# First batch of an attention-plus-FFN kernel: turns, masks and value scaling placed anew

## The chip, the cores and the metric

One core of a Trainium2 chip runs the whole kernel. The metric is device time in microseconds (us) of one launch; medians are given, and every comparison is with runs of the kernel before on the same chip in the same session. Engines are named as in the profile: PE is TensorE (matmuls), ACT is ScalarE, DVE is VectorE, POOL is GpSimd, SP is SyncE.

## The reference, cut to what matters

Attention with a forget gate over 8 batches, 8 heads, 576 positions, 64 channels, and then a gated FFN over the 4608 tokens.

```python
def _attn_ref(q, k, v, f):
    scores = scale * np.matmul(q, k.transpose(0, 1, 3, 2))
    cum = np.cumsum(np.log(np.clip(f, 0.0001, 1.0)), axis=-1)
    scores = np.where(causal, -1000000000.0, scores + decay)   # decay from cum
    ...
    return np.matmul(softmax, v)
# FFN: (sigmoid(x @ w_gate) * (x @ w_val)) @ w_out
```

## The kernel before: the parts that the change touches

The kernel works on one batch after the other; within a batch on four pairs of heads. While batch b+1 is in attention, TensorE fills its time with the FFN of batch b. Only the first batch has no FFN beside it, and only the first batch's schedule is changed. I call the moment when the first transposes of the second batch start on TensorE the **hand-over**: what comes after it is the same in both kernels.

For each pair p of the first batch there are three score units U, V and W. One unit is: scores on TensorE, the exponential on ScalarE, the causal mask (`affine_select`) on GpSimd.

```python
def S_unit(p, u, slot, tag=None, e=None):
    ...                                    # score matmuls into PSUM
    nc.scalar.activation(e[:, :, 0:w], ps[:, sc:sc + 2, 0:w], ACTF.Exp, scale=scale)
    m, pat = diag(e)
    nc.gpsimd.affine_select(out=m, in_=m, compare_op=ALU.is_ge, fill=0.0,
                            base=0, pattern=pat, channel_multiplier=-1)

def vg_step(p, eng=None):                  # values times the gate; GpSimd unless told otherwise
    ...
def out_one(p, bs, bv):
    pair_region(p, 512 * bs, 0, MAIN, False)    # ten matmuls: sums of weights
    ...                                         # VectorE: transpose, reciprocal, spread
    yield
    pair_region(p, 512 * bv, 0, MAIN, True)     # ten matmuls: values (needs vg of p)
    scaled(p, 512 * bv, R, 0, MAIN)
    if p == 0:
        cross_x(p, 1, 0, MAIN)                  # exchange of halves by two transfers
def swap(p, bank):                              # the same exchange by TensorE and a ScalarE copy
    ...

main_unit(0, "U", 0)
for p in range(HPAIR):
    main_unit(p, "V", 1 - p % 2)
    if p + 1 < HPAIR:
        T_step(p + 1, 4, DVEC, ACTC)            # turn q and k of the next pair
    if p:
        burst = out_one(p - 1, 6, 7)
        next(burst)
    main_unit(p, "W", p % 2)
    if p == 0:
        load_qk(1, 0, ((0, 4),))
    elif p == 1:
        load_w1(512, 1024)
    if p > 1:
        vg_step(p)
    if p + 1 < HPAIR:
        main_unit(p + 1, "U", 1 - p % 2)
    if p == 0:
        vg_step(0, nc.vector)
        vg_step(1, nc.vector)
    if p:
        next(burst, None)
load_w1(1024, 1536)
swap(1, 0)
...                                             # FFN projections of the first batch begin
```

In what follows a *turn* is `T_step`, the transposes of one pair's q and k; a *burst* is `out_one`, and its two halves are the *sums* and the *values*; *vg* is the value scaling. The calls are in program order for every engine. `load_qk` and `load_w1` are issued by GpSimd too, two transfers each.

The softmax here doesn't subtract the row's maximum and nothing guards it: scores larger than these inputs give would overflow.

## Time and profile before

| | before |
|---|---|
| median | 374.01 us (373.73 to 374.12, 3 runs) |
| span in the profile | 372.6 us |
| first exponential | 8.85 us |
| pair 2's masks done | 19.53 us |
| hand-over | 28.07 us |
| from hand-over to end | 344.5 us |

The prediction shows the chain. The table of stretches gives, for each stretch in us, its length, the busy time of PE, PEld, DVE, ACT and POOL with instruction counts, then the clock share, the DMA share and GB/s:

```profile
16.80:21.60 4.80, 4.52 (x90) 2.96 (x88) 4.13 (x8) 4.61 (x6) 3.82 (x8) 1.00 1.22 210
21.60:28.10 6.50, 6.25 (x72) 2.80 (x69) 3.87 (x7) 2.60 (x5) 6.50 (x10) 1.00 1.24 210
100.00:200.00 100.00, 99.99 (x1694) 55.04 (x1692) 52.70 (x123) 54.09 (x82) 63.50 (x93) 1.00 1.12 159
```

From 16.8 us on TensorE has 0.5 us of slack before the hand-over, and almost none in the long stretch from 100 to 200 us. In GpSimd's timeline (start, length, engine, line, operation, operands) pair 2's three masks are these:

```profile
17.07 0.43 POOL L250 TENSOR_SCALAR_AFFINE_SELECT gv<-gv 128x256 bf16<-128x256 bf16 x1
18.04 0.64 POOL L250 TENSOR_SCALAR_AFFINE_SELECT gv<-gv 128x512 bf16<-128x512 bf16 x1 [0.54 <-ACT gv L248]
19.12 0.41 POOL L250 TENSOR_SCALAR_AFFINE_SELECT gv<-gv 128x256 bf16<-128x256 bf16 x1 [0.45 <-ACT gv L248]
```

The brackets say that GpSimd was idle before the second and third and waited for their exponentials. These two are as early as ScalarE allows; the first stands directly behind a weight load.

### The profile page before, as it was taken

The page shows a single profiled execution, that of the slowest core. Times are in us where ns is not written, and L with a number is a line of the kernel's source. Part 1 is how long each engine was busy: PE and PEld are TensorE (multiplying, and loading weights), DVE is VectorE, ACT ScalarE, POOL GpSimd, SP SyncE. Part 2 cuts the span into 40 slices and gives each one's busy share as a digit, 9 for nine tenths or more (in the row PEclk, how much of TensorE's full clock was granted, in tenths as well). Part 3 has the DMA queues.
Part 4 walks back from the last instruction along what each step waited for, and adds up shares of the span by engine and source line. Part 5 has one row for each costly group of instructions (what it writes and reads, how often), then busy time and mean ns, then how long its engine had stood idle before and what let it go on. Part 6 is the DMA issues. An engine that isn't in the chain of part 4 may idle for free.

```text
span 372.6 us, 12205 instructions
## 1 busy us (share of the span) xinstructions
PE 359.1 (96%) x5259; PEld 192.5 (52%) x5264; DVE 178.1 (48%) x382; ACT 195.6 (52%) x294; POOL 168.3 (45%) x265
## 2 busy tenths in 40 slices
PE   3899999999999999999999999999999999999996
PEld 1547645455645545454665556544456544444442
DVE  5875473557374755273617460737064703312320
ACT  5858754573637472947285628471747223323321
POOL 8895734134845494959664946460515000000000
PEclk9999999999999999999999999999999999999999
DMA  8999599679999996999993997595313131011002
GB/s 157 233 211 257 88 194 184 187 179 179 196 142 197 171 127 66 203 198 151 147 195 81 199 167 149 126 166 80 97 59 76 32 102 58 3 56 58 0 25 90
DMA packets 101349, 49.24 MB, mean 132 GB/s; under 512 B 72000, under 2 KB 94400, under 8 KB 101296
## 3 DMA queue, kind: packets, MB, share of 16 engines
q0 software_dynamic: 48704, 20.65, 43.5%
q1 hardware_dynamic: 52448, 27.68, 32.1%
q8 instruction: 41, 0.67, 0.7%
q10 hardware_dynamic: 144, 0.13, 0.1%
q14 instruction: 12, 0.10, 0.1%
HBM read 37.90 MB, written 9.44 MB: 127 GB/s over the span
## 4 chain that ended last, share of the span: by engine, by line
PE 93%; ACT 2%; DMA 1%; issue 1%; POOL 1%; DVE 1%; ACTq 0%; POOLq 0%
PE ps L457 51%; PE ps L497 17%; PE ps L506 8%; PE ps L354 8%; PE ps L241 6%; PE ps L195 2%; PE ps L302 1%; DMA qk_in<-in_k_dram 1%; ACT eC L248 0%; ACT eB L248 0%; ACT eA L248 0%; POOL vg L259 0%; POOL gv L250 0%; ACT gv L248 0%; PE ps L419 0%
## 5 line engine op out<-in xcount | busy, mean ns | idle before, releaser
L457 PE MATMUL ps<-xR,w 64*128 64x512 bf16 x1728 | 205.2, 376 | 0.1
L467 DVE SCALAR_TENSOR_TENSOR gv<-sg,ps 128x512 bf16<-128x512 bf16 x108 | 74.1, 687 | 151.8 <-ACT sg L466 148.5
L457 PEld LDWEIGHTS <-w 64*128 64x128 bf16 x1728 | 87.0, 94 | 83.4 <-issue 1.8
L466 ACT ACTIVATE sg<-ps 128x512 bf16<-128x512 f32 x108 | 64.5, 598 | 84.6 <-PE ps L457 83.6
L250 POOL TENSOR_SCALAR_AFFINE_SELECT eC<-eC 128x256 bf16<-128x256 bf16 x31 | 12.6, 407 | 94.9 <-ACT eC L248 90.0
L241 PE MATMUL ps<-qT,kT 64*128 64x320 bf16 (+6 forms) x416 | 48.5, 275 | 1.8 <-ACT kT L200 1.1
L248 ACT ACTIVATE eC<-ps 128x896 bf16<-128x896 f32 (+1 forms) x31 | 27.4, 885 | 20.8 <-PE ps L241 20.5
L259 POOL TENSOR_TENSOR vg<-vb,g_bf 128x640 bf16<-128x640 f32 x30 | 37.9, 1263 | 0.0
L484 ACT ACTIVATE ob<-ps 128x512 f32<-128x512 f32 x35 | 19.6, 596 | 32.1 <-PE ps L506 20.1
L497 PE MATMUL ps<-wox,gvx 64*128 64x512 bf16 x288 | 35.6, 376 | 0.0
L241 PEld LDWEIGHTS <-kT 64*128 64x128 bf16 x416 | 23.3, 96 | 22.9 <-issue 4.2
L497 PE MATMUL ps<-wo,gv 64*128 64x512 bf16 x288 | 34.5, 376 | 0.0
L248 ACT ACTIVATE eA<-ps 128x896 bf16<-128x896 f32 (+2 forms) x32 | 29.4, 922 | 7.7 <-PE ps L241 7.3
L506 PE MATMUL ps<-wo,gv 128*128 128x512 bf16 x140 | 32.1, 380 | 0.3 <-issue 0.2
L248 ACT ACTIVATE eB<-ps 128x768 bf16<-128x768 f32 (+2 forms) x32 | 26.4, 827 | 10.2 <-PE ps L241 9.4
L273 DVE TENSOR_TENSOR xR<-ps,R 128x64 bf16<-128x64 f32 (+2 forms) x68 | 26.2, 429 | 2.5 <-PE ps L302 0.3
L108 POOL DMA_DIRECT2D vb<-in_v_dram x30 | 25.2, 847 | 0.2 <-issue 0.2
L265 DVE STREAM_TRANSPOSE R<-r 128x576 f32<-128x576 f32 (+1 forms) x32 | 24.6, 770 | 1.1
L497 PEld LDWEIGHTS <-gv 64*128 64x128 bf16 x288 | 15.3, 94 | 14.1 <-issue 1.0
L497 PEld LDWEIGHTS <-gvx 64*128 64x128 bf16 x288 | 15.9, 94 | 12.9
L248 ACT ACTIVATE eD<-ps 128x640 bf16<-128x640 f32 x30 | 21.1, 703 | 2.2 <-PE ps L241 2.2
L506 PEld LDWEIGHTS <-gv 128*128 128x128 bf16 x144 | 13.4, 98 | 16.7 <-issue 1.4
(86 smaller groups left out, 329.9 us busy)
## 6 DMA issues: line engine op xcount, KB each, us to landing
out_dram<-ob SPq DMA_DIRECT2D x35, 256.0 KB, 2.2
vb<-in_v_dram POOLq DMA_DIRECT2D x20, 256.0 KB, 5.2
xR<-xR SPq DMA_DIRECT2D x20, 144.0 KB, 3.9
gvx<-gv SPq DMA_DIRECT2D x12, 192.0 KB, 4.2
vb<-in_v_dram SPq DMA_DIRECT2D x8, 256.0 KB, 5.9
k_rows<-in_k_dram POOLq DMA_DIRECT2D x16, 128.0 KB, 5.9
q_rows<-in_q_dram POOLq DMA_DIRECT2D x16, 128.0 KB, 5.3
qk_in<-in_q_dram POOLq DMA_DIRECT2D x7, 288.0 KB, 8.7
```

The source lines that it names most:

```text
L108: eng.dma_start(vbs[b % 2][0:n, t, h0:h1, :], rows)
L241: nc.tensor.matmul(ps[:, sc + h, c:c + i1 - i0], k_at(p, jt)[hp, :], qT[hp, i0:i1], start=True, stop=True)
L248: nc.scalar.activation(e[:, :, 0:w], ps[:, sc:sc + 2, 0:w], ACTF.Exp, scale=scale)
L259: (eng or nc.gpsimd).tensor_tensor(out=vg[:, :, :, 0:D], in0=vbs[b % 2][:, :, 2 * a:2 * a + 2, :], in1=g_bf[:, :, 2 * p:2 * p + 2].unsquee ...
L265: nc.vector.transpose(R.rearrange("p (n c) -> p n c", c=32), r.unsqueeze(2).to_broadcast([128, r.shape[1], 32]))
L273: nc.vector.tensor_tensor(out=xR[:, a, r0:r0 + n], in0=psf[:, o + i:o + i + n], in1=R[:, i:i + n], op=ALU.mult)
L354: nc.tensor.matmul(psf[32 * qd:32 * qd + 32, o + a:o + z], lhsT_of(jt, qd), e_of(u, qd)[:, c:c + z - a], start=(y == 0), stop=(y == len(to ...
L457: nc.tensor.matmul(ps[:, bk, :], w1[half, head, ft * NP:(ft + 1) * NP], xR[half, sl, t0:t0 + TCH], start=(first and x == 0), stop=(last an ...
L466: nc.scalar.activation(sg, ps[:, fb, :], ACTF.Tanh, scale=0.5)
L467: nc.vector.scalar_tensor_tensor(out=gv[:, ft, :], in0=sg, scalar=1.0, in1=ps[:, fb + 1, :], op0=ALU.add, op1=ALU.mult)
L497: nc.tensor.matmul(ps[:, bk, :], lhsT, rhs, start=(x == 0 and ft == 0), stop=(x == 1 and ft == NFT - 1))
L506: nc.tensor.matmul(ps[:, 4 + tt, :], gv[:, ft, tt * NP:(tt + 1) * NP], wo[:, ft, :], start=(ft == 0), stop=(ft == NFT - 1))
```

## The change

It is meant to take work off the busy GpSimd in the first batch and to keep TensorE fed. Pair 3's causal mask becomes a matmul that adds -1e6 to the masked scores; pair 0's halves are exchanged by a fourth `swap`; value scaling of pair 1 goes from VectorE to GpSimd; the third turn, the bursts, the value scaling of pairs 2 and 3 and the weight loads move. The core of the diff:

```diff
+    def mask_block(sc, c):
+        for lhsT, rhs, x in ((ident_bf, tri, 0), (swap_bf, triS, 1)):
+            for h in range(2):
+                ...
+                nc.tensor.matmul(ps[:, sc + h, c:c + n], lhsT[hp, :], rhs[hp, 0:n],
+                                 start=False, stop=True, skip_group_check=True)
...
+            if masked and i0 == jt * NP:
+                mask_block(sc, c)
...
+        if masked:
+            return
...
-        if p == 0:
-            cross_x(p, 1, 0, MAIN)
...
+    nc.gpsimd.affine_select(out=tri, in_=tri, compare_op=ALU.is_ge, fill=-1e6, ...)
...
+        nc.vector.tensor_copy(triS[a, :], tri[b, :])
...                       # the loop is written out; from pair 0's W on:
+    vg_step(0, nc.vector)
+    vg_step(1)
+    load_qk(1, 0, ((0, 4),))
+    main_unit(1, "U", 1)
+    main_unit(1, "V", 0)
+    T_step(2, 4, DVEC, ACTC)
+    half_burst(0)
+    main_unit(1, "W", 1)
+    load_w1(512, 1024)
+    vg_step(2)
+    vg_step(3)
     load_w1(1024, 1536)
+    main_unit(2, "U", 0)
+    half_burst(0)
+    T_step(3, 4, DVEC, ACTC)
+    main_unit(2, "V", 1)
+    main_unit(2, "W", 0)
+    half_burst(1)
+    main_unit(3, "U", 1)
+    half_burst(1)
+    main_unit(3, "V", 0)
+    half_burst(2)
+    main_unit(3, "W", 1)
+    half_burst(2)
+    swap(0, 0)
+    swap(1, 1)
...                       # order of projections, swaps and pair 3's burst
```

More of the change, by code (lines that the diff above doesn't have):

```diff
@@ L78 @@
     xt = gvx[:, 0, :].rearrange("p (a d) -> p a d", d=64)
+    tri, triS = gvx[:, 2, 0:128], gvx[:, 2, 128:256]
     qTs = [single(f"qT{i}", [128, HPAIR, SPAD], BF16) for i in range(2)]
@@ L231, in slot_free, with S_unit @@
             pop_chain()
-    def S_unit(p, u, slot, tag=None, e=None):
+    def mask_block(sc, c):
+        for lhsT, rhs, x in ((ident_bf, tri, 0), (swap_bf, triS, 1)):
+            for h in range(2):
+                hp = slice(64 * h, 64 * h + 64)
+                n = 64 if x == h else NP
+                nc.tensor.matmul(ps[:, sc + h, c:c + n], lhsT[hp, :], rhs[hp, 0:n],
+                                 start=False, stop=True, skip_group_check=True)
+    def S_unit(p, u, slot, tag=None, e=None, masked=False):
         slot_free(slot)
@@ L520, in ffn_step @@
             g2_twin(c, s - 2 * NFT)
+    nc.vector.memset(tri, 0.0)
     nc.sync.dma_start(f_nat, f.rearrange("b h s -> (b h) s"))
@@ L529 @@
     make_identity(nc, ident_f)
+    nc.gpsimd.affine_select(out=tri, in_=tri, compare_op=ALU.is_ge, fill=-1e6,
+                            base=0, pattern=[[1, NP]], channel_multiplier=-1)
     load_v(0, 4, 8, range(NJT), nc.gpsimd)
@@ L558, in main_unit, with half_burst @@
     def main_unit(p, u, slot):
-        S_unit(p, u, slot, e=own[u] if p == 2 else None)
+        S_unit(p, u, slot, e=own[u] if p == 2 else None, masked=p == HPAIR - 1)
+    bursts = [out_one(p, 6, 7) for p in range(HPAIR - 1)] + [out_one(HPAIR - 1, 2, 3)]
+    def half_burst(p):
+        next(bursts[p], None)
     main_unit(0, "U", 0)
-    for p in range(HPAIR):
-        main_unit(p, "V", 1 - p % 2)
-        if p + 1 < HPAIR:
-            T_step(p + 1, 4, DVEC, ACTC)
-        if p:
-            burst = out_one(p - 1, 6, 7)
-            next(burst)
-        main_unit(p, "W", p % 2)
-        if p == 0:
-            load_qk(1, 0, ((0, 4),))
-        elif p == 1:
-            load_w1(512, 1024)
-        if p > 1:
-            vg_step(p)
-        if p + 1 < HPAIR:
-            main_unit(p + 1, "U", 1 - p % 2)
-        if p == 0:
-            vg_step(0, nc.vector)
-            vg_step(1, nc.vector)
-        if p:
-            next(burst, None)
@@ L583 @@
-    load_w1(1024, 1536)
-    swap(1, 0)
-    g1_slots(0, 0, (0, 1), True, False)
-    burst = out_one(HPAIR - 1, 2, 3)
-    next(burst)
+    main_unit(0, "V", 1)
+    T_step(1, 4, DVEC, ACTC)
+    main_unit(0, "W", 0)
+    vg_step(0, nc.vector)
[9 more added lines that the diff above has]
+    vg_step(3)
+    load_w1(1024, 1536)
@@ L588 @@
+    main_unit(2, "U", 0)
[12 more added lines that the diff above has]
+    swap(1, 1)
+    half_burst(3)
+    g1_slots(0, 0, (0, 1, 4, 5), True, False)
+    swap(2, 1)
+    half_burst(3)
+    load_v(1, 0, 8, range(NJT), nc.gpsimd)
     g1_slots(0, 1, (0, 1), True, False)
-    swap(2, 1)
@@ L590 @@
-    next(burst, None)
-    load_v(1, 0, 8, range(NJT), nc.gpsimd)
-    g1_slots(0, 0, (2, 5), False, False)
     S_unit(0, "Z", 0, "D")
-    g1_slots(0, 1, (2, 5), False, False)
-    g1_slots(0, 0, (4, 6), False, False)
+    g1_slots(0, 1, (4, 5), False, False)
+    g1_slots(0, 0, (2,), False, False)
     swap(3, 2)
-    g1_slots(0, 1, (4, 6, 3), False, False)
+    g1_slots(0, 0, (6,), False, False)
+    g1_slots(0, 1, (2, 6, 3), False, False)
     g1_slots(0, 0, (3, 7), False, True)
```

## The prediction

> **What bounds the kernel now.** I read the engine shares first, then the chain of waits, then a timeline of the first 30 us for one engine at a time, because every edit lies there. The page says that TensorE is the bound of the whole:
>
> ```profile
> PE 359.1 (96%) x5259; PEld 192.5 (52%) x5264; DVE 178.1 (48%) x382; ACT 195.6 (52%) x294; POOL 168.3 (45%) x265
> ```
>
> Of the 13.5 us in which TensorE is not busy, the table of stretches puts most ahead of 28 us: it is busy 8.1 us less than the span up to 11.4 us, and from 28.1 to 300 us it is idle for under 2 us. So I call 28.07 us, when the first four transposes of the next batch start (the first work after this change), the **hand-over**. All later work is one dense TensorE stream; a shift of the hand-over should arrive at the end of the kernel nearly unchanged, and the change can hardly do anything else.
>
> What sets the hand-over? The chain of waits in order of time, from the start of pair 2's second exponential (copied without the links in between that are issue time):
>
> ```profile
> 16.95 1.03 ACT gv L248
> ...
> 18.04 0.64 POOL gv L250
> ...
> 19.12 0.41 POOL gv L250
> 19.53 0.18 POOL vg L258
> 19.71 1.20 POOL vg L259
> ...
> 20.96 0.74 PE ps L302 x10
> 21.70 0.32 PE ps L334
> ```
>
> The columns are start, length, engine and line. The reader is to see ScalarE handing to GpSimd (POOL) and GpSimd holding TensorE until 20.96; from there the chain is TensorE up to the hand-over with 0.25 us of idle. GpSimd's own timeline shows why it is so close to being the bound:
>
> ```profile
> 10.92 0.69 POOL L152 DMA_DIRECT2D w<-in_moe_w_val_dram  x1 [0.29 <-DMA qk_in<-in_q_dram]
> 11.61 0.43 POOL L250 TENSOR_SCALAR_AFFINE_SELECT eA<-eA 128x256 bf16<-128x256 bf16 x1
> 11.98 0.65 POOL L250 TENSOR_SCALAR_AFFINE_SELECT eB<-eB 128x512 bf16<-128x512 bf16 x1
> 12.57 0.41 POOL L250 TENSOR_SCALAR_AFFINE_SELECT eC<-eC 128x256 bf16<-128x256 bf16 x1
> 12.93 0.62 POOL L97 DMA_DIRECT2D qk_in<-in_q_dram  x1
> 13.54 0.62 POOL L97 DMA_DIRECT2D qk_in<-in_k_dram  x1
> 14.16 0.43 POOL L250 TENSOR_SCALAR_AFFINE_SELECT eA<-eA 128x256 bf16<-128x256 bf16 x1
> ...
> 19.48 0.23 POOL L258 COPY vg<-g_bf 128x10 bf16<-128x10 bf16 x1
> 19.64 1.26 POOL L259 TENSOR_TENSOR vg<-vb,g_bf 128x640 bf16<-128x640 f32 x1
> 20.86 0.40 POOL L250 TENSOR_SCALAR_AFFINE_SELECT eA<-eA 128x256 bf16<-128x256 bf16 x1
> ```
>
> It does masks, value scaling (vg) and the issue of loads one after the other.[...]
>
> **What the Trainium skill says.** "TensorE: Matmul & The Clock Gate", section "Architectural detail", says that GpSimd works its queue strictly first in, first out; the trace agrees, since the select at 11.61 starts only when the weight load ahead of it is issued, 1.7 us after its exponential ended (9.87). So on GpSimd program order is time order, and I may add durations up. The same page, Part 1, says that the array runs at half clock until one window of about 3.4 us was busy, and falls back after an idle one. The trace agrees on the first: the pair of 128x512 products takes 0.64 us at 13.04 and 15.09, and 0.41 us from 17.46 on. No run here has an idle stretch after that to show the second. "DMA: Bandwidth & Descriptors", section "SWDGE vs HWDGE vs iDMA", says that GpSimd software builds the descriptors of loads that it issues; the 0.62 to 0.72 us per issue in this trace are the price, and it is that price, not the transfer, that counts below.
>
> **The change part by part.**
>
> - *Pair 3's masks to TensorE.* Removes three selects from GpSimd, 1.32 us (11.61 to 12.93 for the same three). Adds 16 small matmuls: U 4, V 8, W 4. Two run side by side in the two halves of the rows; I estimate 0.1 us a pair from the 0.10 us that a 64x128 weight load takes, 0.8 us in all, most of it while TensorE would wait anyway.
> - *Pair 0's halves by TensorE.* Two small transfers off the SyncE queue (nobody waits for them on the chain) against a fourth swap: 0.32 us of TensorE (21.63 to 21.95) and a ScalarE copy of 0.59 us.
> - *vg of pair 1 from VectorE to GpSimd.* VectorE sheds the 2.04 us instruction at 11.63; GpSimd takes on 1.38 us (19.48 to 20.86).
> - *The third mask set-up.* One more select of about 0.3 us before the loads, absorbed by the 0.29 us wait at 10.92; two VectorE copies, about 0.3 us, delay the first exponential a little, with slack before GpSimd gets to it.
> - *Order on GpSimd.* This is the part that I think decides. Before, pair 2's masks come directly after the second weight load. Afterwards the program puts vg of pair 2, vg of pair 3 and the third weight load **ahead of pair 2's masks**. The sum, from 11.61, start to start: masks of pair 0 1.32 (12.93), vg of pair 1 1.38 (14.31), two loads 1.23 (15.54), masks of pair 1 1.32 (16.86), weights 1.36 (18.22), two vg 1.38 + 1.36 (20.96), weights 1.39 (22.35), masks of pair 2 1.32: **23.67 us**. In the kernel before they end at 19.53. Nothing in this list waits for ScalarE: pair 1's last exponential ends at 15.3 and pair 2's at 19.1, so I move them by at most half a microsecond.
>
> Pair 2's sums of weights need those masks and can't start before about 23.75. TensorE works in order; it has pair 3's second scores done at about 20.3 and then has nothing it may do for some 3.4 us. After 23.75 it still owes: sums of pair 2 0.67 (20.96 to 21.63 for such a burst), last scores of pair 3 with their masks 0.35 (estimate from 0.2 for the scores and two pairs of masks), values of pair 2 0.67, two swaps 0.64, sums of pair 3 0.67, 32 projection matmuls at 0.116 (12 of them took 1.39 us from 26.68) 3.7, two more swaps 0.64, values of pair 3 0.67, the remainder's scores 0.14. That is 8.15 us, so the hand-over comes at 31.9 instead of 28.07: **+3.8 us**. With other engines' copies fitting in between (VectorE's chain of 2.4 us after pair 3's sums ends about 29.5, ahead of the swap that needs it at about 30) I take +3.6 to +3.8. What the change saves, three masks off the GpSimd path and 32 projections that wait less, would only count if GpSimd were free by 21.6.
>
> **The rivals.**
>
> - *The change works as intended.* ScalarE then is the bound: its exponentials and copies run from 8.85 to 21.55 with 0.9 us of idle, and pair 3 would follow them without the 0.9 us to the sums at 22.49. After pair 3's last exponential TensorE owes 5.8 us, which gives a hand-over of 27.3: 0.7 us faster, 373.3. For it: less GpSimd work per mask. Against it: the sum above, which uses only measured lengths and in-order issue. It would take an error of 4 us in 12.
> - *TensorE turns cold in its gap.* An idle stretch of 3.4 us is as long as the window that the skill gives. If the clock drops, about 3.4 us of the owed work goes at half rate, 1.7 us more: 379.4. For it: the length; against it: a window would have to lie wholly within the gap. I give it one in four.
> - *A wait for the loads takes over.* GpSimd stalls when old loads are not done (the 0.29 us at 10.92; in the list of waits 1.2 us at 31.28 and 2.2 at 34.09). Each of these three waits is for the load eight places earlier in GpSimd's order; by that count the third weight load waits for a value load that is needed and landed long before, and the loads behind stay in the same order. DMA is saturated up to 36 us in both. I make nothing of it for the time.
> - *The delay is absorbed later.* If after the hand-over some stage waited for loads, 3.7 us of delay would be partly free. The list of waits after 28.1 us shows TensorE with almost none (0.1 us before the 1728 projections), so at most a few tenths.
>
> **Range and chances.** 374.0 + 3.6 = 377.6 as the main case; one in four at 379.4; one in ten near 373.3 to 375. I predict 377.7 us, 375.4 to 380.2 in 8 of 10. Over 2% slower is beyond 381.5, which needs both a cold array and another stall: 0.05. Over 2% faster (366.5) would need 7.5 us from a stretch that has not that much idle: 0.01.
>
> **What would show it.** In the changed kernel's GpSimd timeline: no idle from about 11 to 23.7 us; pair 2's three selects at 22.3 to 23.7, directly behind the third weight load. On TensorE: a gap of 3 to 4 us before the sums that read pair 2's tile, released by GpSimd; the hand-over at 31.5 to 32; product pairs of 128x512 still 0.41 us after the gap (0.64 would be the cold rival). Wrong would be: pair 2's masks before 21 us; a hand-over at or before 28; a total that does not follow the hand-over within half a microsecond.

## The result, and the profile after

| | before | after |
|---|---|---|
| median | 373.87 us (373.09 to 374.12, 4 runs) | 379.36 us (378.94 to 380.20, 4 runs) |
| span in the profile | 372.6 | 377.8 |
| first exponential | 8.85 | 9.18 |
| pair 2's masks done | 19.53 | about 24.1 |
| hand-over | 28.07 | 32.94 |
| from hand-over to end | 344.5 | 344.9 |
| mean granted clock | 1.0 (profile) | 0.989 to 0.995 (timed runs) |

The ratio is 1.0153 (95% interval 1.013 to 1.0177). Ratios here are the mean time of one kernel's fast runs over the mean of the other's of the same rounds, so they differ a little from the ratio of the medians quoted. The changed kernel is 5.5 us slower, within the 2% that counts as the same, and inside the predicted range. The loss lies nearly all ahead of the hand-over: of the 5.2 us between the two profiled spans 4.87 us are in the hand-over, and the rest of the kernel takes the same time to 0.4 us.

First the page's engine shares, to be held against those that the prediction shows of before:

```profile
PE 360.9 (96%) x5281; PEld 191.1 (51%) x5281; DVE 176.6 (47%) x383; ACT 196.2 (52%) x295; POOL 168.4 (45%) x265
```

They tell nothing: GpSimd's share is the same 45%. The chain of waits, in order of time, tells it (start, length, what), and should be read against the one in the prediction:

```profile
17.40 1.31 POOL w L153 x2
18.71 0.23 POOL vg L273
18.94 1.19 POOL vg L274
20.13 0.16 POOL vg L273
20.29 1.18 POOL vg L274
21.48 1.34 POOL w L153 x2
22.82 0.43 POOL gv L265
23.25 0.04 issue
23.29 1.58 PE ps L317 x10
```

Before, GpSimd was in the chain for short pieces between ScalarE's; now it is the chain, without a break: a weight load, two value scalings, another weight load, and only then pair 2's first mask (gv L265). TensorE's timeline around it:

```profile
20.11 0.22 PE L252 MATMUL ps<-qT,kT 64*128 64x128 bf16 x2
23.29 1.58 PE L317 MATMUL ps<-gv,g_bf 128*64 128x512 bf16 x10 [2.96 <-POOL gv L265]
24.81 0.40 PE L252 MATMUL ps<-qT,kT 64*128 64x256 bf16 x2
...
25.29 1.28 PE L317 MATMUL ps<-gv,vg 128*64 128x512 bf16 x10
```

TensorE stands for 2.96 us, released by GpSimd's mask. And then the same ten matmuls take 1.58 us that took 0.74 us in the kernel before:

```profile
19.87 0.74 PE L302 MATMUL ps<-gv,g_bf 128*64 128x512 bf16 x10
```

The table of stretches, one us each, shows why in the third column from the end, the granted clock:

```profile
22.00:23.00 1.00, 0.00 (x0) 0.00 (x0) 0.00 (x0) 0.00 (x0) 1.00 (x3) 1.00 1.23 212
23.00:24.00 1.00, 0.71 (x4) 0.24 (x4) 0.00 (x0) 0.00 (x0) 1.00 (x3) 0.57 1.27 205
24.00:25.00 1.00, 1.00 (x12) 0.55 (x13) 0.09 (x1) 0.00 (x0) 1.00 (x2) 0.50 1.23 206
25.00:26.00 1.00, 1.00 (x12) 0.58 (x10) 0.93 (x3) 0.54 (x1) 1.00 (x3) 0.50 1.24 207
26.00:27.00 1.00, 1.00 (x10) 0.42 (x6) 0.90 (x2) 0.12 (x2) 1.00 (x2) 0.73 1.24 204
27.00:28.00 1.00, 1.00 (x15) 0.64 (x16) 0.56 (x2) 1.00 (x2) 1.00 (x2) 1.00 1.25 208
```

The clock fell to half just as the work came back. By the trace's clock records it was half from 23.14 to 26.55 us, 3.41 us. One thing about this column: the records begin with the first rise (at 16.31 us here), and the view counts everything before it as full clock, although the matmul lengths there (0.64 us for the 512-column pair) say half.

### The profile page after: what moved, and what is told of

It is laid out like the page before. It is cut to its first block, busy times and chain, and to the rows that moved or that the text cites. A ratio compares the mean times of both kernels' runs of the same rounds, so it can differ in the third digit from the quotient of the medians.

```text
span 377.8 us, 12244 instructions
## 1 busy us (share of the span) xinstructions
PE 360.9 (96%) x5281; PEld 191.1 (51%) x5281; DVE 176.6 (47%) x383; ACT 196.2 (52%) x295; POOL 168.4 (45%) x265
## 4 chain that ended last, share of the span: by engine, by line
PE 91%; POOL 4%; DMA 2%; ACT 1%; issue 1%; DVE 0%; POOLq 0%; ACTq 0%
PE ps L470 50%; PE ps L510 16%; PE ps L519 8%; PE ps L367 8%; PE ps L252 5%; DMA qk_in<-in_q_dram 2%; PE ps L196 1%; PE ps L317 1%; POOL qk_in L98 1%; POOL vg L274 1%; POOL w L153 1%; ACT eC L261 0%; POOL eB L265 0%; PE ps L347 0%; ACT eA L261 0%
## 5 line engine op out<-in xcount | busy, mean ns | idle before, releaser
L470 PEld LDWEIGHTS <-w 64*128 64x128 bf16 x1728 | 86.0, 94 | 85.5 <-issue 3.2
L265 POOL TENSOR_SCALAR_AFFINE_SELECT eC<-eC 128x256 bf16<-128x256 bf16 x30 | 12.1, 404 | 98.2 <-ACT eC L261 98.2
L274 POOL TENSOR_TENSOR vg<-vb,g_bf 128x640 bf16<-128x640 f32 x31 | 39.1, 1261 | 0.0
```

Source lines behind the costliest of these rows:

```text
L274: (eng or nc.gpsimd).tensor_tensor(out=vg[:, :, :, 0:D], in0=vbs[b % 2][:, :, 2 * a:2 * a + 2, :], in1=g_bf[:, :, 2 * p:2 * p + 2].unsquee ...
L470: nc.tensor.matmul(ps[:, bk, :], w1[half, head, ft * NP:(ft + 1) * NP], xR[half, sl, t0:t0 + TCH], start=(first and x == 0), stop=(last an ...
```

## The experiments

Two things happened at once: pair 2's masks came late, and the clock fell. And the change has other parts (masks, a fourth swap, another burst order) which could cost time too. **Theory:** the order on GpSimd makes the masks late, the gap that this opens drops the clock, and together they are the whole loss. **Rivals:** the other parts of the change cost the time; GpSimd's total load is the bound, whatever hangs on it; the clock is only a mark and costs nothing.

Single times scatter by up to 1% in these sessions (the kernel before: 373.1 to 376.9), so beside each ratio stands what the profile shows, the time from the first exponential to the hand-over, which takes out most of the differences in when the first loads land:

| run | first exponential | hand-over | difference | ratio to before | mean clock, timed runs |
|---|---|---|---|---|---|
| before | 8.85 | 28.07 | 19.22 | 1 | 0.994 to 1.0 |
| changed kernel | 9.18 | 32.94 | 23.76 | 1.0153 | 0.989 to 0.995 |
| masks of pair 2 first | 9.28 | 29.19 | 19.91 | 0.9996 | 0.998 to 1.0 |
| gap filled | 8.99 | 31.89 | 22.90 | 1.0083 | 0.998 to 1.0 |
| third load late | 9.37 | 32.93 | 23.56 | 1.0094 | 0.994, 0.995 x4, 1.0 |
| before, order alone | 8.84 | 32.32 | 23.48 | 1.0116 | 0.989 to 0.995, one 1.0 |
| pair 2's masks on TensorE | 8.98 | 28.28 | 19.30 | 0.9992 | 0.998 to 1.0 |
| scaling of pair 2 first | 9.21 | 30.08 | 20.87 | 1.0004 | 0.999 to 1.0 |
| before, masks alone | 8.92 | 28.04 | 19.12 | 1.0006 | 0.998 to 1.0 |
| busy start, first trial | 9.29 | 28.87 | 19.58 | 1.0055 | 0.986 to 1.0 |
| order alone, gap filled | 8.87 | 30.45 | 21.58 | 1.0070 | 0.999 to 1.0 |
| third load late, short gap | 9.24 | 31.36 | 22.12 | 1.0046 | 0.998 to 1.0 |
| busy start, second trial | 8.97 | 28.90 | 19.93 | 1.0029 | 0.989 to 0.995 |

In all of them the time from hand-over to the end stays between 343.8 and 345.6 us, so the hand-over decides most of it. All results were correct.

### Undo the order alone: pair 2's masks first

```diff
     load_w1(512, 1024)
-    vg_step(2)
-    vg_step(3)
-    load_w1(1024, 1536)
     main_unit(2, "U", 0)
...
     main_unit(2, "W", 0)
+    vg_step(2)
+    vg_step(3)
+    load_w1(1024, 1536)
```

> The changed kernel with one move: the value scaling of pairs 2 and 3 and the third weight load come after pair 2's masks in GpSimd's order, nothing else. Theory (order on GpSimd, plus the cold clock that its gap brings, is the whole loss): pair 2's masks end near 20.0 us instead of 24.2, no TensorE gap over 1 us, hand-over at 27.3 to 28.3 us, total 373 to 374.3 us. Rival (the added TensorE work, the earlier third transposes or the new burst order cost the time): the hand-over stays beyond 30 us and the total beyond 376 us.

Measured: 374.58 us against 374.79, ratio 0.9996 (0.9974 to 1.0018). The other parts of the change are all still in; the loss is gone. GpSimd's timeline:

```profile
18.63 0.68 POOL L153 DMA_DIRECT2D w<-in_moe_w_val_dram  x1
19.31 1.37 POOL L265 TENSOR_SCALAR_AFFINE_SELECT gv<-gv 128x256 bf16<-128x256 bf16 x3
20.62 0.23 POOL L273 COPY vg<-g_bf 128x10 bf16<-128x10 bf16 x1
20.77 1.26 POOL L274 TENSOR_TENSOR vg<-vb,g_bf 128x640 bf16<-128x640 f32 x1
```

The three masks start at 19.31 instead of 22.82 and no TensorE wait is longer than 0.65 us. The hand-over, 29.19 us, is 0.9 us past what I had expected at most. About 0.6 us of it is one mask in pair 0, which took 1.24 us in this profile (0.65 in the changed kernel's); it ran beside a VectorE scaling that had waited for a late load. The same mask took 1.24 us in one more profile, that of the run with the third load late, again beside such a scaling; that the one caused the other is not shown.

### The clock by itself: fill the gap

Twelve matmuls whose results nobody reads go where TensorE stands; GpSimd's order stays late.

```diff
     main_unit(3, "V", 0)
+    for _ in range(12):
+        nc.tensor.matmul(ps[:, 4, :], ident_bf, qTs[0][:, 0, 0:512], start=True, stop=True)
     half_burst(2)
```

> The changed kernel with 12 idle 128x512 matmuls (results never read) in TensorE's gap before pair 2's sums; the order on GpSimd stays. Theory (the gap lets the clock fall to half, which costs about 1.5 us on top of the late masks: sums 1.52 to 0.67, values 1.21 to 0.67, scores 0.1): masks still end at 24.2, sums of pair 2 0.74 us instead of 1.58, hand-over 31.4 to 31.7 instead of 32.9, total 377.6 to 378.2 us. Rival (the low clock is only a mark in the records, or the surplus over my sum comes from something else): total stays at 379 us or more.

Measured: 378.06 us, ratio 1.0083 (1.0061 to 1.0105), clock 0.998 or more in all six runs. TensorE's timeline:

```profile
19.98 2.76 PE L609 MATMUL ps<-qT,ident_bf 128*128 128x512 bf16 x12
23.21 0.41 PE L317 MATMUL ps<-gv,g_bf 128*64 128x512 bf16 x2 [0.47 <-POOL gv L265]
23.80 0.76 PE L317 MATMUL ps<-gv,g_bf 128*64 128x256 bf16 x8 [0.18 <-POOL gv L265]
24.50 0.28 PE L252 MATMUL ps<-qT,kT 64*128 64x256 bf16 x2
24.80 0.74 PE L317 MATMUL ps<-gv,vg 128*64 128x512 bf16 x10
```

The sums start at the same time as in the changed kernel, the masks being as late as there, but the work behind runs at full clock and the hand-over is about 0.9 us nearer to the first exponential (22.90 against 23.76). The clock does cost time; adding useless work made the kernel faster. The saving in the profile is less than the 1.5 us I had written down, because at full clock the sums overtake GpSimd and wait for the second mask as well (0.18 us before the second line of them). In the ratios to the kernel before (1.0153 and 1.0127 for the changed kernel, 1.0083 here) it is 1.6 to 2.6 us; these come from different sessions, so the size is known only roughly.

### Less in front of the masks: only the third load late

```diff
     vg_step(3)
-    load_w1(1024, 1536)
...
     main_unit(2, "W", 0)
+    load_w1(1024, 1536)
```

> The changed kernel with only the third weight load moved behind pair 2's masks. Theory: masks of pair 2 end 1.39 us earlier, at 22.8; the gap shrinks from 2.96 to about 1.6 us and the clock stays full, so the hand-over comes at about 30.0 and the total at 376.0 to 376.9 us, that is 2.9 us less for 1.39 us of GpSimd time. If the clock has no part: hand-over 31.5, total 378.0 us.

Measured: 378.66 us, ratio 1.0094. A miss. The gap did shrink, to 1.78 us, but the clock fell all the same in five of six runs (0.994 or 0.995), later, from 24.31 to 27.72 us, when TensorE had been back at work for 1.6 us (since 22.72). The fall hits denser work there, so GpSimd's 1.39 us bought almost nothing in the profile (23.56 against 23.76). The sixth run kept a clock of 1.0 and was the fastest, 377.2 us; the others took 377.8 to 379.3. That is the same kernel on the same chip, and so a second sign of what the clock costs. The stretch of 3.41 us that ended with the fall:

```profile
20.90:24.31 3.41, 1.38 (x18) 0.74 (x16) 0.57 (x2) 1.02 (x1) 3.41 (x8) 1.00 1.23 207
```

TensorE was busy for 1.38 us of it, 40%. My expectation that a gap must fill the window was wrong.

### One part alone: the order put into the kernel before

```diff
             load_w1(512, 1024)
+            vg_step(2)
+            vg_step(3)
+            load_w1(1024, 1536)
-        if p > 1:
-            vg_step(p)
...
-    load_w1(1024, 1536)
```

> The kernel before with the order alone: value scaling of pairs 2 and 3 and the third weight load put ahead of pair 2's masks on GpSimd; masks of pair 3 stay on GpSimd, no fourth swap, no other order. Theory: pair 2's masks end at about 22.5 instead of 19.5 us, pair 3's at 23.8, the gap ahead of pair 2's sums is about 2 us, hand-over near 30 us, total 375.3 to 376.7 us. Rival (the loss comes from the other parts of the change): within 0.5 us of the kernel before, 373.5 to 374.4 us.

Measured: 379.63 us, ratio 1.0116 (1.009 to 1.0142). The order alone brings nearly the whole loss, without any other part of the change. It is more than I expected, again by the clock: a gap of 2.22 us,

```profile
22.30 0.41 PE L302 MATMUL ps<-gv,g_bf 128*64 128x512 bf16 x2 [2.22 <-POOL gv L250]
```

and half clock from 23.86 to 27.28 us, after a window in which TensorE was busy for 1.32 of 3.41 us, 39%. The one timed run that kept a clock of 1.0 was the fastest here too, 377.61 us against 378.46 to 380.02.

### The same with the gap filled

```diff
         main_unit(p, "V", 1 - p % 2)
+        if p == 3:
+            for _ in range(9):
+                nc.tensor.matmul(ps[:, 4, :], ident_bf, qTs[0][:, 0, 0:512], start=True, stop=True)
```

> The kernel before with the GpSimd order alone, and nine idle matmuls in the gap that this opens. Theory (the order alone delays the masks, and the clock's fall adds about 1 to 1.5 us to that): clock full, hand-over 30.5 to 31.3 us counted with a first exponential at 8.85, ratio 1.006 to 1.009, against 1.0116 without the idle matmuls. If the clock has no part, 1.0116 stays.

Measured: 376.88 us, ratio 1.0070 (1.004 to 1.0101), clock 0.999 or more. From the first exponential to the hand-over 21.58 us, against 23.48 without the filling and 19.22 in the kernel before: of 4.3 us that the order alone costs in the profile, 1.9 us go with the filling and 2.4 us stay. Up to 0.6 us of the 1.9 is not the clock: in the unfilled run the masks started that much later (21.82 against 21.20), GpSimd having begun later. And the 2.4 us are less than the 3.7 us that the changed kernel loses with its gap filled (22.90 less 19.22). The change also puts pair 1's scaling into GpSimd's queue ahead of these masks, 1.36 us from start to start in the trace; in the changed kernel with its gap filled they start at 22.73 us instead of 21.20. That fits the difference of 1.3 us, but no run has this scaling alone.

### How much idling drops the clock

The run with the third load late, with three filling matmuls at the start of its gap:

```diff
     main_unit(3, "V", 0)
+    for _ in range(3):
+        nc.tensor.matmul(ps[:, 4, :], ident_bf, qTs[0][:, 0, 0:512], start=True, stop=True)
```

> The run with only the third weight load moved, with three idle matmuls at the start of its gap of 1.78 us, leaving about 1.1 us. There the window of 3.41 us that ended with the fall had TensorE idle for 1.5 us of it. Theory (the fall comes from the idle share of one window): 1.1 us is at most a third of a window and the clock stays full, 1.000 in at least four of six runs; ratio about 1.005 to 1.007 instead of 1.0094. If any gap of about 1 us is enough, the clock stays at 0.995 and the ratio at 1.008 or more.

(The 1.5 us of idling in that text is misread: by the line above it was 3.41 less 1.38, 2.0 us.)

Measured: 376.19 us, ratio 1.0046 (1.0014 to 1.0078), clock 0.998 or more in six of six runs. Three matmuls of useless work (two of them are on record, 0.59 us) bring the ratio from 1.0094 to 1.0046 at the same place of the masks (22.22 us against 22.27). If windows of 3.41 us are counted on from the clock's rise at 19.47 us, the one with the gap is

```profile
19.47:22.88 3.41, 2.69 (x42) 1.66 (x40) 2.37 (x4) 2.70 (x4) 3.41 (x7) 1.00 1.22 206
```

busy for 79%. So in these profiles 40% busy dropped the clock and 79% kept it; where between them the edge lies, no run tells, and the busy share may not be all that counts (see the two attempts below).

### Remove the dependence instead of the order

```diff
-        S_unit(p, u, slot, e=own[u] if p == 2 else None, masked=p == HPAIR - 1)
+        S_unit(p, u, slot, e=own[u] if p == 2 else None, masked=p >= HPAIR - 2)
```

> The changed kernel with pair 2's masks on TensorE too; the order on GpSimd is otherwise kept. Theory (what costs is only that pair 2's sums depend on GpSimd work queued late): with the dependence gone the late queue is harmless, ScalarE's exponentials set the pace, no TensorE gap over 1.2 us, clock full, hand-over 27.7 to 28.8 us, ratio to the kernel before 0.996 to 1.001. Rival (GpSimd's total work is the bound whatever hangs on it, through the values of pairs 2 and 3): hand-over beyond 30 us, ratio over 1.005.

Measured: 374.29 us against 374.50, ratio 0.9992 (0.996 to 1.0023). The late GpSimd queue stays, the third weight load is issued at 20.97 as if nothing had changed, and it harms nobody, because pair 2's sums no longer depend on it and have started before:

```profile
20.22 0.73 PE L317 MATMUL ps<-gv,g_bf 128*64 128x512 bf16 x10
```

GpSimd's total load is not the bound; the dependence was. TensorE's longest wait is 0.35 us, for ScalarE.

### Masks on TensorE alone

The kernel before, with only pair 3's masks moved (its order, its transfers and its bursts kept).

```diff
-        S_unit(p, u, slot, e=own[u] if p == 2 else None)
+        S_unit(p, u, slot, e=own[u] if p == 2 else None, masked=p == HPAIR - 1)
```

> The kernel before with one part alone: pair 3's masks by TensorE. Order, exchange by transfer and bursts as before. Theory: masks were not the limit once ScalarE's last exponential is done (sums of pair 3 started 0.9 us after it), so from the first exponential the hand-over comes 0.2 to 0.9 us earlier; ratio 0.9965 to 1.0. Rival (16 added matmuls and the mask set-up cost more than they save): hand-over later, ratio 1.001 or more.

Measured: 374.63 us against 374.50, ratio 1.0006 (0.9972 to 1.0041); 19.12 us from first exponential to hand-over against 19.22. Neither the gain nor the loss shows. From 20 to 24 us TensorE is busy for 3.85 of 4.00 us in this profile: the sums of pair 3 start at 22.38, hardly earlier than before (22.49), not because they wait for a mask but because TensorE is still at the swap and the projections ahead of them.

### Scaling of pair 2 ahead of its masks

On top of the run with pair 2's masks first:

```diff
     main_unit(1, "W", 1)
-    load_w1(512, 1024)
+    vg_step(2)
...
     main_unit(2, "W", 0)
-    vg_step(2)
+    load_w1(512, 1024)
     vg_step(3)
     load_w1(1024, 1536)
```

> As the run with pair 2's masks first, but the value scaling of pair 2 goes ahead of those masks and the second weight load behind them. In that run TensorE stood 0.65 us before pair 2's values, waiting for the scaling. Theory: that wait goes, the masks end no later than 0.2 us after where they did (their exponentials bound them), hand-over 0.4 to 0.7 us earlier counted from the first exponential, ratio to the kernel before 0.9965 to 0.9995. Rival: a later second weight load starves the loads and shows as a wait on them after the hand-over; ratio 1.001 or more.

Measured: ratio 1.0004 (0.9974 to 1.0034). The wait of 0.65 us before pair 2's values is gone, but the profile was disturbed at the start: VectorE waited 1.88 us for a value load, pair 2's first scores came 0.86 us late, and the clock rose only at 19.41 us. Inconclusive for the gain. The rival's starved loads don't show: from hand-over to end it took 343.8 us, the shortest of all.

### Two attempts to have the clock up earlier

Idle matmuls on zeros while TensorE waits for the first loads; on top of the masks of pair 2 on TensorE. First trial: ten at the start. Second: nine at the start, two behind the first two transposes, two before pair 1's scores.

```diff
+    zero = gvx[:, 4:6, :].rearrange("p a c -> p (a c)")
+    nc.vector.memset(zero, 0.0)
+    def keep_busy(n, bank):
+        for _ in range(n):
+            nc.tensor.matmul(ps[:, bank, :], zero[:, 0:128], zero, start=True, stop=True)
+    keep_busy(9, 0)
```

> The run with pair 2's masks on TensorE, and ten idle 128x512 matmuls on zeros while TensorE waits for the first loads. Theory (the clock follows TensorE's activity, and the first batch loses time at half clock up to 16 to 18 us): products before 16 us take 0.41 instead of 0.64 us, hand-over 0.3 to 1.5 us earlier than without, ratio 0.992 to 0.999. If ScalarE and GpSimd alone set the pace there, the hand-over stays and only TensorE's waits grow.

> The run with pair 2's masks on TensorE and idle matmuls on zeros at the start, this time also in the two later gaps (behind the first two transposes, and before pair 1's first scores), so that no 3.4 us stretch from 1.3 us on has more than 0.5 us idle. Theory: the clock is full by 11 us, products before 16 us take 0.41 us, hand-over 0.5 to 1.5 us earlier from the first exponential than the 19.3 us without; ratio 0.994 to 0.998. If matmuls on zeros don't count as activity, the clock rises at 16 to 18 us as before and the ratio is 1.000 or more, as in the first trial (1.0055).

Measured: ratios 1.0055 (1.0022 to 1.0088) and 1.0029 (0.999 to 1.0068). Neither works. In the first trial's profile the clock rose only at 17.32 us. In the second it was full at 7.17 us, so matmuls on zeros do count, but it fell again at 10.58 and came back at 17.41. The stretch that ended with that fall:

```profile
7.17:10.58 3.41, 2.29 (x70) 1.51 (x63) 2.36 (x6) 2.39 (x4) 3.41 (x6) 1.00 1.22 216
```

By TensorE's busy time it was 67% full, but 59 of its 70 matmuls were transposes of 64x64. That transposes count for less is what the Trainium skill says ("TensorE: Matmul & The Clock Gate", Part 4). The first trial points the same way: in its window from 7.08 to 10.49 us, counted back from the rise, TensorE was busy for 3.20 of 3.41 us, 94%, and the clock did not rise, while windows of 91% (scaling of pair 2 first, 15.99 to 19.41) and 93% (second trial, 3.76 to 7.17) raised it. 75 of its 85 matmuls were transposes. Whether it is that they are transposes or that they are small, no run separates.

Why the first trial lost as much as 0.5% with a hand-over only 0.3 us later than without is open in part. In its profile 0.9 us lie after the hand-over, in one TensorE pause of 1.9 us between 200 and 250 us that the profile puts down to no wait (1.0 us in the run with pair 2's masks on TensorE). And four of the six timed runs had a mean clock of 0.986 to 0.994, which points to falls that this profile doesn't have.

### The changed kernel once more

> The changed kernel unaltered, timed again on the same chip as the runs beside it. Theory: mean clock 0.995 or less in every run (one 3.4 us window at half clock), ratio 1.012 to 1.018. If the clock falls only in some runs, the times split into two groups about 1.5 us apart.

Measured: 379.44 us, ratio 1.0127 (1.0097 to 1.0158). The clock fell in every run; three runs show 0.994 or 0.995 (378.5 to 379.3 us) and three 0.989 or 0.990 (379.6 to 380.2 us). A single fall of 3.41 us at half clock takes 3.41 / 377 / 2 = 0.0045 off the mean, so the second three fit two such windows at half clock; no trace of such a run was kept. The profile, of a run at 0.995, repeats the first one: 23.70 us from the first exponential to the hand-over, half clock from 23.10 to 26.52. The kernel before is not free of it either: its slowest run beside these, 376.93 us, is its only one with a clock as low as 0.994. No version tried beats the kernel before by more than the noise.

## Why the prediction was right, and where its sizes were off

**The main step held.** The text said that the program puts two value scalings and a weight load ahead of pair 2's masks on an engine that works in order, and summed the work to 12.06 us from pair 0's first mask to the end of pair 2's. The trace has 12.1 us (12.08 to about 24.1). Undoing the order removed the loss, doing it alone in the kernel before brought a loss of 1.2%, of the 1.3 to 1.5% of the whole change: shown. The predicted consequences on TensorE are there too: a gap of 3 us, released by GpSimd, and no recovery later (344.5 and 344.9 us after the hand-over).

**The term that was mis-sized is the clock.** The text held a cold array in the gap possible but gave it "one in four", because "a window would have to lie wholly within the gap". That step failed. The clock fell in all ten timed runs of the changed kernel, and in ten of twelve runs with gaps of 1.78 and 2.22 us, well under a window: a window that was 40% busy sufficed. The size given for it, 1.7 us, was near enough (about 0.9 us in the profile, where late masks cover part of it, 1.6 to 2.6 us in the ratios). With the gap filled the loss from the first exponential to the hand-over is 3.7 us (22.90 less 19.22), which is the main case's 3.6 to 3.8; the measured 379.36 us is the rival's 379.4. That the first agrees so well is part luck: with the gap filled the sums began 14.2 us after the first exponential (23.21 less 8.99) where the text had 14.9 (23.75 less 8.85), and from there TensorE owed 8.7 us (23.21 to 31.89) where the text had 8.15.

**Smaller steps were off.** Pair 2's sums were said to start after all three masks, at 23.75; they started after the first, at 23.29, because the matmuls that read the first unit come first. And the third mask set-up was said to vanish in a wait of 0.29 us; in the profile of the changed kernel that wait was still there (0.30 us) and GpSimd's masks began at 12.08 instead of 11.61. But in the other runs with the same set-up they began anywhere from 11.6 to 12.5, and without it from 11.6 to 12.0, so this is mostly when the first loads land and not the change. Three readings of the kernel before are wrong, without weight for the result: TensorE is busy 7.6 us less than the span up to 11.4 us (8.1 us less up to 28.1), ScalarE's idling from 8.85 to 21.55 is 1.1 us and not 0.9, and the 0.25 us of idle in the chain is the swap without a record.

**What would have been gained was overstated.** The rival "works as intended" promised 0.7 us once GpSimd is out of the way. With pair 2's masks on TensorE it was out of the way and the ratio is 0.9992, the hand-over 19.30 us after the first exponential against 19.22. The text had counted ScalarE's last exponential as what TensorE waits for. But TensorE had no long wait there: it starts pair 3's sums about where it did before (22.39 against 22.49), and after them it owes 5.9 us instead of 5.6 to the hand-over, with four projection matmuls more, because ahead of the sums the added swap has taken their place. GpSimd was relieved of masks by an engine that had no more room than it. That the other parts are worth nothing in this place is shown within some 0.3%; finer than that these runs don't reach.

**The change by its parts**, as far as the runs separate them: order on GpSimd, about 3.7 us of the time to the hand-over in the changed kernel, of which 2.4 us come with the order alone and the rest fits pair 1's scaling in the same queue (it costs nothing once the masks go first); clock, about 1 us more in the profile; masks on TensorE, turns, fourth swap and burst order together, nothing that can be seen.

## What to carry to other kernels

On an engine that works in order, ask of each instruction not what it costs but who waits for what stands behind it: nearly the same work, at the same busy share, cost 1.5%, the clock's part included, because three short masks were queued behind 4.1 us of work (18.70 to 22.82) of which nothing was needed before them. And do not book a TensorE gap at its own length: in this kernel a gap of under 2 us was enough to put the next, densest stretch at half clock, and a few useless matmuls in the gap were cheaper than the idling. Before moving work off a busy engine, check that it is on the path and that the engine that takes it is not.

## What the Trainium skill lacked or had wrong

- "TensorE: Matmul & The Clock Gate", Part 1, puts the fall to half clock after at least one idle window of about 3.4 us. The window's length agrees: half clock lasted 3.41 us, and the clock's rise and fall are two such lengths apart (16.31 and 23.14). But the window need not be idle: it fell after windows in which TensorE was busy 40% (1.38 of 3.41 us) and 39% (1.32, in the kernel before with the order alone), and stayed after one of 79%. The page also tells of short idle pieces that make the clock swing, but gives no share.
- The same page's table of advice warns of gaps over about 3 us. Gaps of 1.78 and 2.22 us dropped the clock here in ten of twelve runs.
- The same page does not spell out that the fall comes at the window's end, on work that may have resumed already: TensorE was back at 22.72 us and lost the clock at 24.31 (third load late).
- "DMA: Bandwidth & Descriptors", the section on the anatomy of one DMA on the GpSimd path, calls the generation of descriptors small and variable in the time of a transfer. For the engine that does it it is not small: 0.62 to 0.76 us for a load of q, k or FFN weights in the changed kernel (144 to 512 KB), in order with its other work, so the six loads between 12 and 24 us held GpSimd for 4.0 us.
